# One core's pooled attention with a max-of-two MoE behind it: PE's order from a list scheduler, score groups in bursts, the first K transposed on PE

## The chip, the cores and the metric

The kernel runs on one core of a Trainium2 chip. The metric is device time in microseconds (us) of one execution, as the median of several runs. Engines are named as in the profile: PE (TensorE, matrix products), DVE (VectorE), ACT (ScalarE), POOL (GpSimd) and SP (SyncE, which issues every DMA of this kernel, in order).

## What is computed

Eight batches, eight heads, 1152 keys, head size 64. Queries are averaged in pairs first, so each head has 576 of them. The attention output of all heads, 4608 tokens of 512 values, goes through a small MoE layer.

```python
q_pool = q.reshape(B, H, S // 2, 2, D).mean(axis=3)
scores = np.matmul(q_pool, k.transpose(0, 1, 3, 2)) / np.sqrt(D)
attn = softmax(scores)                      # over the 1152 keys
x = np.matmul(attn, v)                      # -> 4608 x 512
h1, h2 = x @ w1, x @ w2                     # 512 -> 1024
out = np.maximum(h1, h2) @ w_out            # 1024 -> 512
```

The kernel writes max(h1, h2) as relu(x (w1 - w2)) + x w2, so it needs wd = w1 - w2 and w21 = w2 w_out, and never h2 itself.

## The kernel before

A *pair* is two heads of one batch, so there are 32 pairs, four to a batch. A pair is loaded by three DMAs of 576 KB (K, Q, V); POOL casts K to bf16 (L222), adds neighbouring queries (L228) and casts V into vE, which has a column of ones for the softmax sums (L232). K is transposed by a DMA from SP (L225), the pooled Q by six PE transposes and a DVE copy (`qtrans`, L243, L249).

Scores come out transposed, keys on partitions. A *score group* (`scores`) is one tile of 128 keys against 512 queries for both heads, two matmuls in one half each of PE's rows (L263), followed by one exp of 1024 columns on ACT (L275). After nine of these come two groups for the last 64 queries: eight key tiles at once (16 matmuls, one wide exp) and the ninth (2 matmuls, a short exp, L287). That is 11 groups per pair, 352 in all. The groups use two PSUM tiles in turn (`sps`, two banks each).

The product with V (`av_units`) is eight *chunks* of nine matmuls (L305), 128 queries of one head each, and one *rest* of nine for the last 64 queries of both heads (L317), into two banks `av`. DVE divides by the sums (L329 to L345) into xnat. When the fourth pair of a batch is done, five DMA transposes turn xnat into xT (`xtrans`, L369).

The MoE works on blocks of 512 tokens, nine in all, each of which needs the xT of one or two batches. A block is eight hidden units of four matmuls (`hid`, L449) with a relu on DVE (L461), and four output tiles of twelve matmuls (`proj`, L482) with a copy (L496) and two or three stores (L433). In the last blocks ACT takes half of the evacuations (L456, L493). MoE, w21 (L415) and the Q transposes share two banks `mps`.

All instructions are recorded in one program order by class `Plan`, which derives the semaphore waits from the names that an operation reads and writes; each engine then executes its own operations in that order. The order is written out at the end of the function: the loads, casts and transposes of pairs 0 and 1, then all weights (`w_load`), the first Q transpose, then pair by pair the 11 score groups, between which the AV units of the pair before and up to six MoE units are spread by estimated costs. A block enters the queue of MoE units one pair after its last batch is complete, whether or not its xT has landed. So SP's queue begins with the loads of pairs 0 and 1, goes on with w2, its four transposes (L392), w_out and w1, and DVE's with the casts of w2 and w_out and the four subtractions for wd (L403); the copy of the first transposed Q (L249) comes after those.

Of the kernel before, what the change touches and what calls it, by code (L numbers as in the profile page):

```python
# [7 lines left out]
P = 128  # L8
# [5 lines left out]
class Plan:  # L14
# [13 lines left out]
    def op(self, eng, fn, r=(), w=(), dma=None):  # L28
        n = len(self.ops)
        deps = set()  # L30
        raw = set()
        for k in r:
            if k in self.writer:
                deps.add(self.writer[k])
                raw.add(self.writer[k])
# [4 lines left out]
        deps.discard(n)  # L40
        self.ops.append(dict(eng=eng, fn=fn, deps=deps, raw=raw, dma=dma, w=tuple(w)))
# [68 lines left out]

def bass_funnel_attn__then__act_maxout2_kernel(
# [14 lines left out]
    QP = 96  # L126
# [15 lines left out]
    with ctx:  # L142
# [6 lines left out]
        ident = sbuf([QP, QP], BF16, "ident")  # L149
# [19 lines left out]
        w2f = xT[:, :, NTOK - 4096:NTOK - 2048].bitcast(FP32)  # L169
        w2b = xT[:, :, NTOK - 1024:NTOK]  # L170
        w2T = xT[:, :, NTOK - 2048:NTOK - 1024].rearrange("p c (f x) -> p c f x", x=P)
# [11 lines left out]

        mcount = [0]

        def next_m():
            m = mcount[0] % 2
            mcount[0] += 1
            return m

        def setup():
            def ones(g):
# [7 lines left out]
                ident[:, :], ident[:, :], pattern=[[1, QP]], compare_op=ALU.is_equal,  # L200
                fill=0.0, base=0, channel_multiplier=-1), r=["id0"], w=["ident"])

        def load(i):
            b, h0 = i // NHP, 2 * (i % NHP)
            s = i % 2
# [3 lines left out]
                w=[f"kraw{s}"], dma=f"d_k{s}")  # L209
# [3 lines left out]
                w=[f"qraw{s}"], dma=f"d_q{s}")  # L213
# [3 lines left out]
                w=[f"vraw{s}"], dma=f"d_v{s}")  # L217

        def cast(i):
# [3 lines left out]
                kbf[s][:, :, :, :].rearrange("p t h d -> p h t d"), kraw[s][:, :, :, :],  # L223
                1.0, 1.0, ALU.mult, ALU.mult), r=[f"kraw{s}"], w=[f"kbf{s}"])
            op("SP", lambda e: e.dma_start_transpose(  # L225
                kT[v3][:, :, :], kbf[s][:, :, :, :].rearrange("p t h d -> p (t h d)")),
                r=[f"kbf{s}"], w=[f"kT{v3}"], dma=f"d_kT{v3}")
            op("POOL", lambda g: g.tensor_tensor(  # L228
                qp[s][:, :, :, :].rearrange("p u h d -> p h u d"),
                qraw[s][:, :, :, 0, :], qraw[s][:, :, :, 1, :], ALU.add),  # L230
                r=[f"qraw{s}"], w=[f"qp{s}"])
            op("POOL", lambda g: g.tensor_scalar(  # L232
                vE[v3][:, :, :, 0:D].rearrange("p t h d -> p h t d"), vraw[s][:, :, :, :],
                1.0, 1.0, ALU.mult, ALU.mult), r=[f"vraw{s}"], w=[f"vE{v3}"])

        def qtrans(i):
            s = i % 2
            m = next_m()
            mb = mps[m][:, :].bitcast(BF16)

            def pe(e):
                for u in range(QU):
                    last = e.transpose(  # L243
                        mb[:, u * QP:(u + 1) * QP],
                        qp[s][:, u, :, :].rearrange("p h d -> p (h d)"), ident[:, :])
                return last

            op("PE", pe, r=[f"qp{s}", "ident"], w=[f"m{m}"])
            op("DVE", lambda e: e.tensor_copy(qpT[s][:, :], mb[:, 0:SQ]),  # L249
               r=[f"m{m}"], w=[f"qpT{s}", f"m{m}"])  # L250

        gcount = [0]

        def scores(i, g):
# [3 lines left out]
            r = gcount[0] % 2  # L258
# [33 lines left out]
            op("PE", pe, r=[f"kT{ks}", f"qpT{qs}"], w=[f"s{r}"])  # L292
            op("ACT", act, r=[f"s{r}"], w=[w, f"s{r}"])

        def av_units(i):
            b, h0 = i // NHP, 2 * (i % NHP)
            es = i % 2
            vs = i % 3
            xs = b % 2
            c0 = h0 * D  # L300

            def chunk(half, sb):
                def pe(e):
                    for t in range(NT):
                        last = e.matmul(  # L305
                            av[half][:, sb * 66:sb * 66 + 65],
                            eta[es][:, half, t, sb * P:(sb + 1) * P],
                            vE[vs][:, t, half, 0:65],
                            start=(t == 0), stop=(t == NT - 1))
                    return last  # L310
                op("PE", pe, r=[f"eta{es}.{t}" for t in range(NT)] + [f"vE{vs}"],
                   w=[f"av{half}"])

            def rest():
                def pe(e):
                    for t in range(NT):
                        last = e.matmul(  # L317
                            av[0][:, 4 * 66:4 * 66 + 131],
# [197 lines left out]
        for i in range(NPAIR):  # L516
            if i + 2 < NPAIR:
                load(i + 2)
# [87 lines left out]
```

## Time and profile before

| | us |
|---|---|
| median of 3 runs | 530.05 |
| lowest and highest | 528.51, 531.62 |
| the profiled execution | 530.39 |
| its span, first to last instruction | 528.7 |
| PE busy in it | 423.2 |
| ACT busy in it | 325.0 |
| DVE busy, POOL busy | 151.0, 133.3 |

The profile is of one execution; the time that it took and the span of its instructions stand in the table. Busy time counts an engine as working from an instruction's start to its end. Matmuls overlap, so their cost is better read as the distance from one start to the next. The stretches that matter are the beginning, where no scores run yet, the 32 pairs, in which scores, AV and MoE mix, and the end, where two MoE blocks run alone.

### The profile page before, as it was taken

How to read it: one execution, taken by the hardware profiler on the slowest of the kernel's cores; microseconds unless marked ns; L12 is line 12 of the kernel's file. 1: busy time of each engine (PE TensorE's matmuls, PEld its weight loads, DVE VectorE, ACT ScalarE, POOL GpSimd, SP SyncE). 2: the span in 40 equal slices, each digit the busy share in tenths (PEclk: the TensorE clock that was granted, in tenths of full speed). 3: DMA queues.
4: the chain of work that ended last, by engine and by line, in shares of the span. 5: the costliest groups of instructions: out<-in, count | busy, mean ns of one | idle time of the engine just before them, and what ended most of it. 6: DMA issues, size and time to landing. Idle time of an engine off the chain costs nothing.

```text
span 528.7 us, 10621 instructions
## 1 busy us (share of the span) xinstructions
PE 423.2 (80%) x4688; PEld 209.7 (40%) x4688; DVE 151.0 (29%) x330; ACT 325.0 (61%) x365; POOL 133.3 (25%) x105
## 2 busy tenths in 40 slices
PE   0000789849994999789986999799979997899997
PEld 0000245424452445334543455354435443445443
DVE  0107023204222432233222423242224322423221
ACT  0000887937784677757783779477847786674120
POOL 4204233305033233323241422152405032300000
PEclk9999999979997899979997999799979998999999
DMA  8799856049287939975877879695859496702423
GB/s 237 234 274 351 223 149 152 12 112 249 84 207 149 275 45 212 198 190 150 179 217 182 179 170 192 151 241 150 225 131 249 119 200 126 177 21 51 70 65 81
DMA packets 93790, 88.26 MB, mean 167 GB/s; under 512 B 64560, under 2 KB 64560, under 8 KB 93744
## 3 DMA queue, kind: packets, MB, share of 16 engines
q1 hardware_dynamic: 93744, 87.58, 68.4%
q8 instruction: 37, 0.61, 0.5%
q14 instruction: 9, 0.07, 0.0%
HBM read 62.91 MB, written 9.44 MB: 137 GB/s over the span
## 4 chain that ended last, share of the span: by engine, by line
PE 62%; ACT 13%; DMA 13%; SPq 7%; DVE 3%; issue 1%; POOL 0%
PE mps L482 16%; PE sps L263 15%; PE av L305 13%; PE mps L449 13%; ACT eta L275 13%; SPq L369 4%; DMA kT<-kbf 4%; DMA xT<-xnat 3%; PE av L317 2%; DMA stage<-in_moe_w_dram 2%; DMA kraw<-in_k_dram 2%; DVE wd L403 2%; DMA xT<-in_moe_w_dram 2%; PE mps L415 1%; PE mps L243 1%; SPq L392 1%
## 5 line engine op out<-in xcount | busy, mean ns | idle before, releaser
L275 ACT ACTIVATE eta<-sps 128x1024 bf16<-128x1024 f32 x288 | 279.2, 1028 | 157.4 <-PE sps L263 154.5
L263 PE MATMUL sps<-qpT,kT 64*128 64x64 bf16 (+1 forms) x1152 | 136.8, 300 | 62.3 <-DVE qpT L249 43.4
L305 PE MATMUL av<-vE,eta 128*128 128x65 bf16 x2304 | 110.6, 197 | 0.0
L449 PE MATMUL mps<-xT,wd 128*128 128x512 bf16 x288 | 80.7, 413 | 30.1 <-DMA xT<-xnat 30.1
L305 PEld LDWEIGHTS av<-vE,eta 128*128 128x128 bf16 x2304 | 85.0, 99 | 41.9 <-issue 39.8
L263 PEld LDWEIGHTS sps<-qpT,kT 64*128 64x128 bf16 x1152 | 40.1, 94 | 147.9 <-DVE qpT L249 43.6
L222 POOL TENSOR_SCALAR kbf<-kraw 128x1152 bf16<-128x1152 f32 x32 | 38.1, 1191 | 179.7 <-DMA kraw<-in_k_dram 179.7
L461 DVE TENSOR_SCALAR stage<-mps 128x512 bf16<-128x512 f32 x64 | 44.3, 692 | 114.5 <-PE mps L449 114.4
L482 PE MATMUL mps<-wo,stage 128*128 128x512 bf16 x288 | 72.8, 380 | 0.0
L228 POOL TENSOR_TENSOR qp<-qraw 96x768 bf16<-96x768 f32 x32 | 58.1, 1816 | 37.6 <-DMA qraw<-in_q_dram 30.5
L232 POOL TENSOR_SCALAR vE<-vraw 128x1152 bf16<-128x1152 f32 x32 | 36.8, 1150 | 107.4 <-PE av L305 107.4
L449 PEld LDWEIGHTS mps<-xT,wd 128*128 128x128 bf16 x288 | 25.0, 103 | 59.9 <-DMA xT<-xnat 31.4
L496 DVE COPY stage<-mps 128x512 f32<-128x512 f32 x32 | 22.1, 692 | 73.1 <-PE mps L482 73.1
L287 ACT ACTIVATE etb<-sps 128x1024 bf16<-128x1024 f32 x64 | 38.5, 657 | 7.0 <-PE sps L263 7.0
L482 PE MATMUL mps<-w,xT 128*128 128x512 bf16 x144 | 37.1, 380 | 0.0
L329 DVE RECIPROCAL rc<-av 128x6 f32<-128x6 f32 x64 | 12.1, 189 | 87.5 <-PE av L317 69.8
L482 PEld LDWEIGHTS mps<-wo,stage 128*128 128x128 bf16 x288 | 23.9, 98 | 29.6 <-issue 8.6
L249 DVE COPY qpT<-mps 128x576 bf16<-128x576 bf16 x32 | 14.6, 457 | 46.5 <-PE mps L243 46.5
L333 DVE TENSOR_TENSOR xnat<-av,rc 128x256 bf16<-128x256 f32 x64 | 27.2, 424 | 2.2
L317 PE MATMUL av<-vE,etb 128*128 128x131 bf16 x288 | 22.3, 221 | 0.0
L243 PE MATMUL mps<-ident,qp 96*128 96x96 bf16 x192 | 14.1, 212 | 9.3 <-POOL qp L228 9.3
L317 PEld LDWEIGHTS av<-vE,etb 128*128 128x128 bf16 x288 | 16.9, 97 | 5.9 <-issue 5.9
(20 smaller groups left out, 75.1 us busy)
## 6 DMA issues: line engine op xcount, KB each, us to landing
kraw<-in_k_dram SPq DMA_DIRECT2D x32, 576.0 KB, 5.9
qraw<-in_q_dram SPq DMA_DIRECT2D x32, 576.0 KB, 7.8
vraw<-in_v_dram SPq DMA_DIRECT2D x32, 576.0 KB, 8.4
out_dram<-stage SPq DMA_DIRECT2D x24, 192.0 KB, 2.3
out_dram<-stage SPq DMA_DIRECT2D x24, 128.0 KB, 2.5
xT<-in_moe_w_dram SPq DMA_DIRECT2D x1, 2048.0 KB, 8.1
stage<-in_moe_w_out_dram SPq DMA_DIRECT2D x1, 2048.0 KB, 8.6
stage<-in_moe_w_dram SPq DMA_DIRECT2D x1, 2048.0 KB, 13.1
```

Of the source, the lines that this page charges most:

```text
L222: op("POOL", lambda g: g.tensor_scalar(kbf[s][:, :, :, :].rearrange("p t h d -> p h t d"), kraw[s][:, :, :, :], 1.0, 1.0, ALU.mult, ALU.mu ...
L228: op("POOL", lambda g: g.tensor_tensor(qp[s][:, :, :, :].rearrange("p u h d -> p h u d"), qraw[s][:, :, :, 0, :], qraw[s][:, :, :, 1, :], ...
L232: op("POOL", lambda g: g.tensor_scalar(vE[v3][:, :, :, 0:D].rearrange("p t h d -> p h t d"), vraw[s][:, :, :, :], 1.0, 1.0, ALU.mult, ALU. ...
L263: return e.matmul(sps[r][:, half, col:col + n], kT[ks][h:h + 64, t, :], qpT[qs][h:h + 64, lo:lo + n], start=True, stop=True)
L275: return e.activation(eta[es][:, :, g, :], sps[r][:, :, :], EXP, scale=scale)
L287: return e.activation(etb[es][:, t0:t0 + n, :, :].rearrange("p t h c -> p h t c"), sps[r][:, :, 0:n * NB].rearrange("p h (t c) -> p h t c" ...
L305: last = e.matmul(av[half][:, sb * 66:sb * 66 + 65], eta[es][:, half, t, sb * P:(sb + 1) * P], vE[vs][:, t, half, 0:65], start=(t == 0), s ...
L317: last = e.matmul(av[0][:, 4 * 66:4 * 66 + 131], etb[es][:, t, :, :].rearrange("p h c -> p (h c)"), vE[vs][:, t, :, :].rearrange("p h c -> ...
L333: op("DVE", lambda e: e.tensor_tensor(xnat[xs][:, 0:NCH, c:c + D], a[:, 0:NCH * 66].rearrange("p (j c) -> p j c", c=66)[:, :, 0:D], rc[hal ...
L449: last = e.matmul(mps[m][:, :], wd[:, ct, ft * P:(ft + 1) * P], xT[:, ct, n0:n0 + 512], start=(ct == 0), stop=(ct == NC_ - 1))
L461: op("DVE", lambda e: e.tensor_scalar_max(gT[gs][:, ft, :], mps[m][:, :], 0.0), r=[f"m{m}"], w=[f"gT{gs}.{ft}", f"m{m}"])
L482: last = e.matmul(mps[m][:, :], lhs, rhs, start=(part == 0 and j == 0), stop=(part == 2 and j == 3))
```

## The change

PE's order is no longer written out but made by a list scheduler. `Plan.op` now takes a cost and keeps a clock per engine and for the DMA engines, so that `Plan.when` can say when an operation could start. PE's work is put into *jobs* of small units. Two *lanes*, each with one of two PSUM banks `fb`, hold one job at a time; a hidden unit is now two halves of two matmuls, an output tile six units of two. In each step the main loop either emits a burst of two or three score groups, if they can run without a planned stall and ACT's planned lead is short, or the next unit of a lane. Score groups have three PSUM tiles in turn instead of two; `av` and `mps` are gone.

K of pairs 0 to 4 is transposed on PE in two jobs each (`ktrans_pe`), with a DVE copy behind each; later ones by DMA as before. w2 is transposed on PE too (four jobs of eight transposes). w2, w_out and w1 are loaded when pairs 0, 1 and 3 begin, and cast in smaller pieces when the plan sees them landed. K and Q are loaded three pairs ahead and cast two ahead, V two and one; Q of pair 0 is loaded ahead of K, and K of pair 0 is cast on DVE. The transposes to xT and the stores are put into SP's order when the plan sees their data ready. A MoE block is taken up when the plan sees its xT landed and no older block is left.

The core of the diff:

```diff
+    LAT = {"PE": 0.16, "ACT": 0.13, "DVE": 0.1, "POOL": 0.05}
...
+    def when(self, eng, r=(), w=()):
+
+        t = self.free.get(eng, 0.0)
+        for d in self.deps(r, w)[0]:
+            p = self.ops[d]
+            if p["eng"] != eng or p["dma"] is not None:
+                t = max(t, p["seen"] + 0.05)
+        return t
+
...
-        sps = [psum([P, 2, 512], f"sps{g}") for g in range(2)]
-        av = [psum([P, 512], f"av{g}") for g in range(2)]
-        mps = [psum([P, 512], f"mps{g}") for g in range(2)]
+        sps = [psum([P, 2, 512], f"sps{g}") for g in range(3)]
+        fb = [psum([P, 512], f"fb{g}") for g in range(2)]
...
+        def ktrans_pe(i):
+            s = i % 2
+            v3 = i % 3
...
+                def go(e, m, lo=lo, hi=hi):
+                    mb = fb[m][:, :].bitcast(BF16)
+                    for t in range(lo, hi):
+                        last = e.transpose(
+                            mb[:, (t - lo) * P:(t - lo + 1) * P],
+                            kbf[s][:, t, :, :].rearrange("p h d -> p (h d)"), ident[:, :])
+                    return last
+
+                def evac(m, lo=lo, hi=hi):
+                    mb = fb[m][:, :].bitcast(BF16)
+                    dve(lambda e: e.tensor_copy(
+                        kT[v3][:, lo:hi, :].rearrange("p t x -> p (t x)"),
+                        mb[:, 0:(hi - lo) * P]),
+                        [f"f{m}"], [f"kT{v3}", f"f{m}"], 0.7)
+                jobs.append(Job("q", [unit([f"kbf{s}", "ident"], 0.055 * (hi - lo), go)], evac,
+                                ("k", i) if lo else None))
+            return jobs
+
...
         def xtrans(b):
             xs = b % 2
...
                 n0 = b * SQ + j * P
+                under = [key for key, lo, hi in (("w2b", 512, 1536), ("w2T", 1536, 2560),
+                                                 ("w2f", 2560, NTOK))
+                         if n0 < hi and lo < n0 + rows]
                 op("SP", lambda e, rows=rows, n0=n0, j=j: e.dma_start_transpose(
                     xT[:, :, n0:n0 + rows], xnat[xs][0:rows, j, :]),
-                    r=[f"xn{xs}.{j}.{h}" for h in range(H)], 
-                    w=[f"xT.{b}.{j}"] + (["w2f", "w2b", "w2T"] if n0 == 0 else []),
-                    dma=f"d_x{xs}{j}")
+                    r=[f"xn{xs}.{j}.{h}" for h in range(H)],
+                    w=[f"xT.{b}.{j}"] + under,
+                    dma=f"d_x{xs}{j}", cost=0.95, mode="t")
...
-        def moe_units(nb, tail):
+        def moe_jobs(nb, tail):
...
+                def part(kk, ft=ft):
+                    def go(e, m):
+                        for ct in (2 * kk, 2 * kk + 1):
                             last = e.matmul(
-                                mps[m][:, :], wd[:, ct, ft * P:(ft + 1) * P],
+                                fb[m][:, :], wd[:, ct, ft * P:(ft + 1) * P],
                                 xT[:, ct, n0:n0 + 512],
                                 start=(ct == 0), stop=(ct == NC_ - 1))
                         return last
-                    op("PE", pe, r=["wd"] + xkeys(n0, n0 + 512), w=[f"m{m}"])
+                    return unit(["wd"] + xkeys(n0, n0 + 512), 0.432, go)
+
...
+        BURST = 3
+        pe_cost = [0.22] * NT + [0.24, 0.04]
+        act_cost = [0.953] * (NT + 1) + [0.21]
+        groups = [(i, g) for i in range(NPAIR) for g in range(NG)]
+        nxt = 0
+        entered = -1
+        lane = [None, None]
+        av_queue = []
+        q_queue = []
+        w_queue = []
+        moe_queue = []
+        blocks = [((512 * (nb + 1) - 1) // SQ, nb) for nb in range(NBLK)]
+        q_done = set()
+        k_done = set()
+        KPE = 5
+        W_AT = (0, 1, 3)
...
+        def start_k(i):
+            force(("k", i - 2))
+            cast_k(i)
+            if i < KPE:
+                q_queue.extend(ktrans_pe(i))
+            else:
+                later(f"kbf{i % 2}", lambda: (ktrans(i), k_done.add(i)), ("k", i))
+
+        def enter(i):
+            if i + 2 < NPAIR:
+                start_k(i + 2)
+                cast_q(i + 2)
+            if i + 1 < NPAIR:
+                cast_v(i + 1)
+                q_queue.append(qtrans(i + 1))
+            if i + 3 < NPAIR:
+                load_k(i + 3)
+                load_q(i + 3)
+            if i + 2 < NPAIR:
+                load_v(i + 2)
+            if i in W_AT:
+                n = W_AT.index(i)
+                w_load(n)
+
+                def ready():
+                    w_cast(n)
+                    if n == 0:
+                        w_queue.extend(w2t_jobs())
+                    if n == 1:
+                        w_queue.extend(w21_jobs())
+                later(("w2f", "wof", "w1f")[n], ready)
+
...
+        def av_open():
+
+            job, at = av_queue[0]
+            return nxt >= at and plan.when("PE", r=job.units[0][0]) <= now() + 0.1
+
+        def refill():
+
+            if q_queue and plan.when("PE", r=q_queue[0].units[0][0]) <= now():
+                return q_queue.pop(0)
+            if av_queue and (av_open() or nxt >= len(groups)):
+                return av_queue.pop(0)[0]
+            if w_queue and plan.when("PE", r=w_queue[0].units[0][0]) <= now():
+                return w_queue.pop(0)
+            if not moe_queue and blocks and blocks[0][0] in x_done:
+                nb = blocks[0][1]
+                if plan.when("PE", r=xkeys(nb * 512, nb * 512 + 512)) <= now() or nxt >= len(groups):
+                    moe_queue.extend(moe_jobs(blocks.pop(0)[1], nxt >= len(groups)))
+            if moe_queue:
+                if moe_queue[0].kind == "p" and any(l and l.kind == "h" for l in lane):
+                    return None
+                return moe_queue.pop(0)
+            return None
+
+        def burst_now(size):
+
+            todo_g = groups[nxt:nxt + size]
+            if not todo_g:
+                return None, 0.0
+            for p, g in todo_g:
+                if p not in q_done or p not in k_done:
+                    return None, 0.0
+                if p >= 2 and p - 2 not in av_done:
+                    return None, 0.0
+            t = now() + 0.1
+            stall = 0.0
+            n = gcount[0]
+            for kk, (p, g) in enumerate(todo_g):
+                s = plan.when("PE", r=[f"kT{p % 3}", f"qpT{p % 2}"], w=[f"s{(n + kk) % 3}"])
+                stall += max(0.0, s - t)
+                t = max(t, s) + pe_cost[g]
+            return todo_g, stall
+
+        av_done = set()
+
...
+        load_q(0)
+        load_k(0)
+        cast_k(0)
+        cast_q(0)
+        q_queue.extend([qtrans(0)] + ktrans_pe(0))
+        load_k(1)
+        load_q(1)
+        load_v(0)
+        start_k(1)
+        cast_q(1)
+        cast_v(0)
+        load_k(2)
+        load_q(2)
+        load_v(1)
+        turn = 0
+        while nxt < len(groups) or av_queue or moe_queue or blocks or any(lane) or x_wait:
+            flush()
+            lead = plan.free.get("ACT", 0.0) - now()
+            ready = None
+            for size in (3, 2):
+                ready, stall = burst_now(size)
+                if ready and stall <= 0.05:
+                    break
+            first = 0.55
+            for kk in (0, 1):
+                if lane[kk] is None:
+                    lane[kk] = refill()
+            best = None
+            for kk in (turn, 1 - turn):
+                if lane[kk] is not None:
+                    t = plan.when("PE", r=lane[kk].units[0][0], w=[f"f{kk}"])
+                    if best is None or t < best[0] - 0.02:
+                        best = (t, kk, t + lane[kk].units[0][2] - now())
+            if ready and stall <= 0.05 and (best is None or lead < first + best[2]):
+                emit_burst(ready)
+            elif best is not None and (not ready or best[0] <= now() + stall):
+                emit_unit(best[1])
+                turn = 1 - best[1]
+            elif ready:
+                emit_burst(ready)
+            else:
+                plan.free["PE"] = now() + 0.05
+                assert now() < 2000.0, (nxt, entered, lane)
+        plan.free["PE"] = 1e9
+        flush()
 
         plan.solve()
         engines, dmas = plan.sems()
```

## Rows read from the trace of the kernel before

**Rows 1.** The page, part 1: busy time, share of the span and instructions of each engine.

```profile
PE 423.2 (80%) x4688; PEld 209.7 (40%) x4688; DVE 151.0 (29%) x330; ACT 325.0 (61%) x365; POOL 133.3 (25%) x105
```

**Rows 2.** The chain of waits in order of time: start us, us, what.

```profile
0.81 4.39 DMA kraw<-in_k_dram
...
15.04 8.09 DMA xT<-in_moe_w_dram
...
31.52 13.10 DMA stage<-in_moe_w_dram
...
44.65 8.29 DVE wd L403 x4
...
54.02 7.44 ACT eta L275 x8
...
65.83 0.54 PE sps L263
```

**Rows 3.** Timeline of ACT, pair 4: start us, us, engine, line, operation, count, idle before.

```profile
98.55 8.36 ACT L275 ACTIVATE eta<-sps 128x1024 bf16<-128x1024 f32 x9 [0.32 <-PE sps L263]
...
108.31 1.02 ACT L275 ACTIVATE eta<-sps 128x1024 bf16<-128x1024 f32 x1 [0.32 <-PE sps L263]
```

**Rows 4.** Timeline of PE in a pair with MoE work, 128.8 to 141.5 us.

```profile
130.97 0.45 PE L305 MATMUL av<-vE,eta 128*128 128x65 bf16 x9
131.25 1.03 PE L449 MATMUL mps<-xT,wd 128*128 128x512 bf16 x4
132.21 0.39 PE L263 MATMUL sps<-qpT,kT 64*128 64x512 bf16 x2
132.53 0.45 PE L305 MATMUL av<-vE,eta 128*128 128x65 bf16 x9
132.91 0.39 PE L263 MATMUL sps<-qpT,kT 64*128 64x512 bf16 x2
133.24 0.70 PE L317 MATMUL av<-vE,etb 128*128 128x131 bf16 x9
133.77 1.02 PE L482 MATMUL mps<-w,xT 128*128 128x512 bf16 x4
...
137.05 0.43 PE L243 MATMUL mps<-ident,qp 96*128 96x96 bf16 x6
137.31 0.44 PE L305 MATMUL av<-vE,eta 128*128 128x65 bf16 x9
...
138.97 0.41 PE L263 MATMUL sps<-qpT,kT 64*128 64x64 bf16 x16
139.31 0.72 PE L305 MATMUL av<-vE,eta 128*128 128x65 bf16 x18
```

**Rows 5.** By stretches: us, busy us (x instructions) of each engine, granted clock, DMA.

```profile
88.80:108.30 19.50, 16.00 (x249) 9.31 (x248) 4.64 (x15) 18.87 (x23) 6.70 (x6) 1.00 0.22 47
108.30:114.60 6.30, 0.34 (x9) 0.22 (x8) 0.00 (x0) 1.02 (x1) 0.48 (x1) 0.77 0.42 83
114.60:118.50 3.90, 3.86 (x24) 1.51 (x25) 0.69 (x1) 1.26 (x2) 0.00 (x0) 0.50 0.72 205
489.40:524.90 35.50, 35.47 (x160) 14.84 (x160) 8.30 (x12) 6.53 (x11) 0.00 (x0) 1.00 0.34 70
```

**Rows 6.** Waits: engine, line, released by: us in total, times, longest us.

```profile
PE mps L449 <- DMA xT<-xnat: 30.1, 8, 6.0
```

**Rows 7.** Timeline of SP's queue, end of the first batch.

```profile
108.25 6.41 SPq L369 DMA_TRANSPOSE xT<-xnat  x5
```

**Rows 8.** Timeline of PE, two score groups in a row, 80.4 to 81.6 us.

```profile
80.45 0.61 PE L263 MATMUL sps<-qpT,kT 64*128 64x512 bf16 x4
80.99 0.70 PE L317 MATMUL av<-vE,etb 128*128 128x131 bf16 x9
```

**Rows 9.** Timeline of the first 16 us: POOL's add of Q.

```profile
7.43 1.79 POOL L228 TENSOR_TENSOR qp<-qraw 96x768 bf16<-96x768 f32 x1 [1.00 <-DMA qraw<-in_q_dram]
```

**Rows 10.** The page, part 3: DMA queue, packets, MB, share of 16 engines.

```profile
q1 hardware_dynamic: 93744, 87.58, 68.4%
```

More of the change, by code (lines that the diff above doesn't have):

```diff
@@ L26, in __init__, with deps @@
         self.readers = {}
[L28 to L35, printed above, removed]
+        self.free = {}
+        self.dma_free = 0.0
+        self.mode = None
+    def deps(self, r, w):
+        raw = {self.writer[k] for k in r if k in self.writer}
+        deps = set(raw)
         for k in w:
@@ L364, in xtrans @@
+            op("PE", pe, r=[f"kT{ks}", f"qpT{qs}"], w=[f"s{r}"],
+               cost=pe_cost[g], mode="s")
+            op("ACT", act, r=[f"s{r}"], w=[w, f"s{r}"], cost=act_cost[g])
         def xtrans(b):
@@ L419, in go, with evac @@
-                    op("DVE", lambda e: e.tensor_copy(w21[:, ct, :], mps[m][:, :]),
-                       r=[f"m{m}"], w=["w21", f"m{m}"])
-                units.append((1.71, go))
-            return units
+                    return unit([f"w2T{ct}", "wo", "w2T"], 0.432, go)
+                def evac(m, ct=ct):
+                    dve(lambda e: e.tensor_copy(w21[:, ct, :], fb[m][:, :]),
+                        [f"f{m}"], ["w21", f"f{m}"], 0.63)
+                jobs.append(Job("w", [part(kk) for kk in range(4)], evac))
@@ L424, in bass_funnel_attn__then__act_maxout2_kernel @@
+            return jobs
         ocount = [0]
+        held = {}
         def store(t, s):
@@ L546, in bass_funnel_attn__then__act_maxout2_kernel, with part, go @@
[L546 to L552 removed]
+                c0 = n0 + nt * P
+                def part(kk, nt=nt, c0=c0):
+                    def go(e, m):
+                        for j in (2 * kk, 2 * kk + 1):
+                            if j < NC_:
+                                lhs, rhs = xT[:, j, c0:c0 + P], w21[:, j, :]
+                            else:
+                                ft = j - NC_
+                                lhs = gT[gs][:, ft, nt * P:(nt + 1) * P]
+                                rhs = wo[:, ft, :]
+                            last = e.matmul(fb[m][:, :], lhs, rhs,
+                                            start=(j == 0), stop=(j == NC_ + NF - 1))
+                        return last
+                    rd = (["w21"] + xkeys(c0, c0 + P)) if kk < 2 else (
+                        ["wo", f"gT{gs}.{2 * kk - 4}", f"gT{gs}.{2 * kk - 3}"])
+                    return unit(rd, 0.432, go)
@@ new lines, in evac @@
+                def evac(m, nt=nt):
+                    o = ocount[0] % 3
+                    ocount[0] += 1
+                    if o in held:
+                        store(*held.pop(o))
+                    if tail and nt % 2:
+                        op("ACT", lambda e: e.copy(osb[o][:, :], fb[m][:, :]),
+                           r=[f"f{m}"], w=[f"osb{o}", f"f{m}"], cost=0.55)
+                    else:
+                        dve(lambda e: e.tensor_copy(osb[o][:, :], fb[m][:, :]),
+                            [f"f{m}"], [f"osb{o}", f"f{m}"], 0.63)
+                    held[o] = (nb * 4 + nt, o)
@@ new lines, in moe_jobs @@
+                jobs.append(Job("p", [part(kk) for kk in range(6)], evac))
+            return jobs
+        NG = NT + 2
+        BURST = 3
[10 more added lines that the diff above has]
+        blocks = [((512 * (nb + 1) - 1) // SQ, nb) for nb in range(NBLK)]
@@ new lines, in now, with flush @@
+        def now():
+            return plan.free.get("PE", 0.0)
+        def flush():
+            for entry in list(todo):
+                if plan.ops[entry[0]]["seen"] <= now():
+                    todo.remove(entry)
+                    entry[1]()
+            for o in list(held):
+                if plan.ops[plan.writer[f"osb{o}"]]["seen"] <= now():
+                    store(*held.pop(o))
+            for b in list(x_wait):
+                xs = b % 2
+                if plan.ops[plan.writer[f"xn{xs}.{NCH - 1}.{H - 1}"]]["seen"] <= now():
+                    x_wait.remove(b)
+                    xtrans(b)
+                    x_done.add(b)
```

448 lines of the change are left out of this document (222 added, 226 removed).

## The prediction

> **What bounds the kernel now.** I read the page's busy shares first. TensorE (PE) is busy for 80% of the span and no other engine comes near [rows 1], so the first question is what PE does in the other 20%, and the second is what its busy time consists of. The chain of waits answers the first for the beginning: the first exp runs at 54.02 us. Ahead of it stand the load of K (0.81 us, 4.39 long), and then, in one SP queue, w2 (8.09), w_out and w1 (13.10); the chain ends in the subtraction that makes wd on VectorE, from 44.65 to 52.94, behind which the copy of the first transposed Q stands in the DVE queue [rows 2]. Nothing of attention needs wd. The ACT timeline shows what a pair costs where ACT is the limit: from 98.55 to 108.31, 9.76 us for 11 score groups [rows 3]. The PE timeline of a pair with MoE work shows the other limit: there PE has no pause at all and the pair takes 12.7 us (its nine 1024-wide exps would need 9.76). In it nearly every score group stands alone between other matmuls [rows 4]. Finally the view by stretches shows a stall where a batch ends: from 108.30 to 114.60 PE works 0.34 us, and the next 3.9 us run at granted clock 0.50, the 1.2 GHz level, instead of 1.00 [rows 5]. The view of waits puts 30.1 us in 8 such stops on the xT transposes [rows 6]; the SP row shows why: the five transposes of a batch hold SP for 6.41 us [rows 7], and the first MoE block is next in PE's order, ahead of the scores that could have run.
>
> **Prices of PE work, from starts of neighbouring rows.** A score group alone takes 0.32 to the next start, two in a row 0.54 [rows 4, 8], so one group is 0.22 and leaving a run of scores costs 0.10. A chunk ahead of other matmuls takes 0.28, ahead of a score group 0.38: entering a run costs 0.10. So each run of scores pays 0.20 on top. The wide rest group is 0.34 - 0.10 = 0.24, the last one (2 matmuls for 16) 0.03, the 9 "rest" matmuls 0.53, a Q transpose 0.26 [rows 4]. A pair's attention is 9 x 0.22 + 0.24 + 0.03 + 8 x 0.28 + 0.53 + 0.26 = 5.28 us; 32 pairs are 169.0. A MoE block is 20 units of four matmuls at 0.96 - 0.10 = 0.86, 17.2 us; the last two, with nothing else beside them, take 35.50 together [rows 5]: 7 x 17.2 + 35.5 = 155.9. w21 is 8 such units, 6.9. Sum of the work kept: 331.8.
>
> **The change, part by part.**
> *Start.* The weights leave the way: w2, w_out and w1 are loaded at pairs 0, 1 and 3. Q is issued first, then K. The first load of before lands at 5.20, the second, of the same size, at 7.4, when POOL's add of Q starts [rows 2, 9]; with the order turned round K is there at 7.4. Its cast on DVE is about 1 (estimate: half of a wd piece, 2.07 for two inputs), nine transposes and their copies about 1.5. First scores at 10, first exp at 10.5 instead of 54.02. Bounds 9 (cast and transposes of the first half overlap) and 14 (K as late again as the 4.39 of a load, because five loads are now queued at once).
> *Transposes on PE.* 5 x 9 for K and 4 x 8 for w2, 77 of 128 columns. Six of 96 columns take 0.26, so one is 0.058: 4.5 us, bounds 3.4 (0.044) to 9 (six at half clock, 0.116 each). They take 5 K transposes and 4 w2 transposes out of SP's queue; after the start nothing waited for those for long, so I count no gain. The DVE copies they add (14) lie beside PE's two filler banks.
> The Trainium skill, TensorE: Matmul & The Clock Gate, Part 4: PE-mode transpose, puts a 128x128 transpose at about 275 ns inside a kernel; by that figure the 77 would cost 21 us, and the forecast would be 419. The trace disagrees with it for a row of transposes, six in 0.26 us, so it gets no chance of its own.
> *Bursts.* 352 score groups are now in 317 runs (counted in the PE timeline; the rows show the pattern): 63 us of entering and leaving. With three PSUM groups PE can write two while ACT still reads the third. A burst of three fits only where ACT has nearly run dry, since the third group needs the bank that ACT is reading; with fillers at hand the scheduler meets that rarely. Twos alone are 176 x 0.20 = 35, threes alone 24; I take 33. This is 30 us less of PE.
> *Batch ends.* A block's first unit is put into PE's order only when the plan sees its xT landed, and scores go ahead. PE then has MoE work for every free slot: attention leaves 9.76 - 5.28 - 1.03 = 3.45 us per pair, 14 per batch, and a block brings 17.2, so a backlog grows and later blocks start long after their xT. I count the 30.1 us of stops and the half-clock stretches behind them as gone. What is late next: at the first batch nothing is in the backlog. Batch 0 ends at 10.5 + 4 x 9.76 = 49.5; AV of its last pair is released at the sixth group after that (55), the norm ends near 57, the transposes take 6.4 and a landing: first MoE unit at 66.
> *The early gap.* From 10 to 66 PE has 5.7 pairs of scores (5.7 x 3.3 = 18.8), 4.7 of AV (12.8), Q transposes (1.7), the added transposes and w21 (11.4): 44.7 of 56. So 11 us idle, and about 3 more because PE starts at the lower level (at 65.83 the chain still has 0.54 for a score group up to the next start, where 0.32 is normal [rows 2, 4]). 14, bounds 8 to 20.
> *Waits in the queues.* PE runs its order as written; where a real transfer or copy is later than planned, everything behind it waits. The plan has 1.2 for a wd piece; wd took 8.29 for four here [rows 2], 2.07 each. DVE is FIFO, so around pair 4 the Q copy and the norms stand behind wd by up to 6 us. The deeper prefetch gives K and Q about one pair (10 us) of slack for that, and an SP queue held by five transposes delays loads by 6.41 only [rows 7]. Not visible before is how often such a slip reaches PE: bounds 0 and 37 (all stops of before again, 30.1 and some 7 for K and others). I take 3, near the lower end, since in the attention phase PE itself is the slow part and its inputs run ahead.
> *End.* From PE's last start to the span's end 3.8 (528.7 - 524.9 [rows 5]), unchanged.
>
> **Sum.** 10 + 331.8 + 4.5 + 33 + 14 + 3 + 3.8 = 400.1 us of span. The profiled execution took 530.39 with a span of 528.7, so 1.7 lie around it; the median of the runs, 530.05, is 0.3 below that execution, which I ignore. Forecast: 402 us.
>
> **A second way through.** ACT alone would end attention at 10.5 + 32 x 9.76 = 323; behind it come the last AV (2.7), norm and first transpose (about 4), two blocks (35.5) and 3.8: 369. PE's ledger is 31 us longer, so attention may end as late as 354 before it costs anything.
>
> **Rivals.**
> *B, the DMA engines pace attention.* All transfers of before took 68.4% of 16 engines' span, 361.6 us [rows 10]. Of 87.58 MB the change drops about 2.5 (nine transposes), 10 us, and some 12 belong to the last stores: 339 us must pass before attention ends. With the engines full that is 340, under the 354, and costs nothing; at a share of 0.92 it is 369 + 46 = 415, at 0.85 it is 399 + 46 = 445. It decides from a share under 0.96. For it: the stretch without loads in pairs 3 and 4 had a share of 0.22 [rows 5], so SP does leave holes. Against: in that stretch SP sat in front of the transposes of 108.25 [rows 7], waiting for the batch's last norm with the next loads queued behind; the change puts transposes into SP's order only when the plan sees the norm done, and loads two to three pairs ahead. Time 412 to 440, taken as 416.
> *C, the stops come back.* The plan's transfer times are too short, PE waits for xT or K at each batch end and falls to the lower level again: 8 x 3.8 of stop and 8 x about 3.4 of lost clock (half of 6 to 7 us at 0.50) is 58: 460. Against it the backlog, which covers all batches but the first.
> *D, slower than before: half clock through attention.* At the lower level a pair's 5.28 of matmuls become 10.56, with 1.03 of switching 11.6 against 6.3: 5.3 more per pair, and MoE units in such a pair double as well. PE's ledger reaches 530 when 25 of the 32 pairs run so; with all 32 it gives 402 + 170 = 572. It needs PE's short pauses between bursts to be enough to lose the clock. Pairs 3 and 4 of before have just such pauses, PE busy 16.00 of 19.50 us, and the granted clock is 1.00 [rows 5].
> The Trainium skill, TensorE: Matmul & The Clock Gate, A second HAM failure mode: psum-queue depth-cycling, reports a kernel whose short pauses between groups, while it cycles through PSUM banks, make the clock swing; that would be this rival, here from the three-group ring. By that rule the time would be up to the 572; the trace disagrees so far.
> *E, the change doesn't do what it says:* bursts come out as single groups and PE keeps 63 instead of 33: 432, inside the upper part of the range. *F, better than I think:* threes throughout, no early cold: 400.1 - 9 - 6 - 3 + 1.7 = 384.
>
> **How the numbers follow.** My forecast (386 to 412) has 0.60; B 0.20; C 0.08; D 0.03; E 0.04; F 0.05. The range goes from 386 to 436, which leaves out F, C, D and a little of B, about 0.18. A measurement of this kernel tells about 0.5% from no change. Only D and the far end of C reach 527.5: faster 0.96, same 0.01, slower 0.03.
>
> **What would show it.** First exp near 10.5 in the ACT timeline; score runs of four or six matmuls in PE's, some 170 of them; no wait of PE on xT over 2 us after the first block; granted clock 1.00 from about 25 us to the end; attention's last exp between 323 and 354, then 46 to 75 us of MoE alone. If PE is idle for over 30 us between 66 us and the end, the sum was wrong in its waits; if the last exp comes after 360 with DMA at a share under 0.95, B holds.

## The result, and the profile after

The changed kernel takes 435.71 us (median of 4 runs, 435.1 to 439.74); the kernel before took 529.77 beside it. The ratio is 0.825, 95% interval 0.819 to 0.831: 17.5% faster. The forecast was 402, so 34 us of the expected 128 are missing. The time lies at the very end of the range of 386 to 436, and as a ratio (0.825, where 436 of 530.05 is 0.823) just outside it. The profiled execution took 439.74 with a span of 438.0. Its page answers to [rows 1] and [rows 10] (busy time, share, instructions; then the queue's packets, MB, share of 16 engines):

```profile
PE 388.1 (89%) x4714; PEld 205.9 (47%) x4765; DVE 152.7 (35%) x351; ACT 313.1 (71%) x365; POOL 130.4 (30%) x104
...
q1 hardware_dynamic: 83600, 85.05, 78.0%
```

What went as planned is in the timelines of ACT and of PE (start, us, engine, line, work, count, idle before). ACT starts at 11.03 instead of 54.02 [rows 2], and nine K transposes in a row on PE cost 1.05 from their start to the next, at half clock, 0.12 each.

```profile
11.03 8.56 ACT L406 ACTIVATE eta<-sps 128x1024 bf16<-128x1024 f32 x9 [8.95 <-PE sps L394]
```
```profile
16.61 1.12 PE L308 MATMUL fb<-ident,kbf 128*128 128x128 bf16 x9
17.66 1.04 PE L394 MATMUL sps<-qpT,kT 64*128 64x512 bf16 x18
```

What did not is in two stretches (columns as in [rows 5]): up to the last exp at 379.9, and MoE alone. DMA is busy 0.86 of the first. The second has 51 us; from the last exp to the end of the span it is 58, near the short end of the forecast's 46 to 75.

```profile
11.00:382.00 371.00, 335.41 (x4461) 183.78 (x4506) 134.63 (x321) 304.67 (x352) 126.61 (x93) 0.96 0.86 214
382.00:433.00 51.00, 49.78 (x240) 20.75 (x242) 15.32 (x26) 6.53 (x11) 0.00 (x0) 1.00 0.25 64
```

PE's waits on xT [rows 6] are gone from the waits view. But SP's queue has a new line at its top, a transpose that waits for a transpose (engine, line, released by: us, times, longest):

```profile
SPq L435 <- DMA xT<-xnat: 47.1, 26, 8.2
```

To compare whole kernels I add up PE's distances between starts of neighbouring matmuls: to each its price from the prediction (0.216 per 512-wide matmul and so on), 0.105 for each step into or out of a run of scores, the same work once more where the granted clock was 0.50, and what is left over 0.06 is idle. 51 matmul records are missing in the profile of after (4714 against 4765 weight loads); their 11.0 us are put back from idle into work. "Early gap" is idle plus half clock up to 80 us. Work and switching are therefore counts times the prediction's prices; what tests the prices is the rounding line, by which they overstate. The table is of the profiled executions: after's is 4.0 us above its median and e7's 2.5 below, so what an edit is worth is better read from the medians below.

| us | forecast | after | e6 | e12 | e7 | e8 |
|---|---|---|---|---|---|---|
| first matmul | 10 (first scores) | 7.9 | 7.4 | 7.6 | 7.6 | 7.5 |
| work, with added transposes | 336.3 | 334.5 | 334.4 | 334.4 | 334.4 | 335.3 |
| in and out of score runs | 33 | 32.8 | 32.8 | 32.8 | 33.2 | 58.4 |
| early gap: idle + half clock to 80 us | 14 | 15.2 + 10.2 | 15.1 + 7.9 | 13.9 + 10.0 | 14.3 + 9.0 | 12.7 + 6.8 |
| later idle + half clock | 3 | 27.7 + 8.0 | 15.5 + 1.8 | 15.4 + 3.1 | 8.5 + 0 | 9.4 + 0 |
| rounding | | -3.2 | -1.9 | -2.2 | -2.6 | -2.8 |
| last start to end | 3.8 | 5.1 | 4.7 | 4.7 | 5.1 | 4.7 |
| span | 400.1 | 438.0 | 417.6 | 419.7 | 409.5 | 432.1 |

Work, switching and the end are within 2 us of the forecast. The miss is in two lines: 11 in the early gap, 33 later. Of the 11, 1.8 lie before the first scores at 10.4, which the forecast's first line contains.

### The profile page after: what moved, and what is told of

It is laid out like the page before. It is cut to its first block, busy times and chain, and to the rows that moved or that the text cites. A ratio compares the mean times of both kernels' runs of the same rounds, so it can differ in the third digit from the quotient of the medians.

```text
span 438.0 us, 10776 instructions
## 1 busy us (share of the span) xinstructions
PE 388.1 (89%) x4714; PEld 205.9 (47%) x4765; DVE 152.7 (35%) x351; ACT 313.1 (71%) x365; POOL 130.4 (30%) x104
## 3 DMA queue, kind: packets, MB, share of 16 engines
q1 hardware_dynamic: 83600, 85.05, 78.0%
## 4 chain that ended last, share of the span: by engine, by line
PE 64%; DMA 15%; DVE 7%; ACT 6%; SPq 3%; issue 2%; POOL 1%; DVEq 0%
PE fb L571 17%; PE fb L333 15%; PE sps L394 13%; PE fb L541 13%; ACT eta L406 6%; DMA xT<-xnat 4%; DMA kT<-kbf 4%; PE fb L344 4%; DMA qraw<-in_q_dram 3%; DMA out_dram<-stage 3%; DVE stage L555 2%; DVE xnat L361 2%; DVE stage L587 1%; SPq L256 1%; SPq L435 1%
## 5 line engine op out<-in xcount | busy, mean ns | idle before, releaser
L394 PE MATMUL sps<-qpT,kT 64*128 64x64 bf16 (+1 forms) x1152 | 108.0, 298 | 12.5 <-ACT eta L406 6.1
L333 PE MATMUL fb<-vE,eta 128*128 128x65 bf16 x2304 | 97.0, 199 | 11.9 <-DVE stage L587 11.2
L333 PEld LDWEIGHTS fb<-vE,eta 128*128 128x128 bf16 x2304 | 86.5, 101 | 37.8 <-DVE stage L587 12.4
L249 POOL TENSOR_SCALAR kbf<-kraw 128x1152 bf16<-128x1152 f32 x31 | 35.7, 1150 | 159.7 <-DMA kraw<-in_k_dram 159.7
L541 PE MATMUL fb<-xT,wd 128*128 128x512 bf16 x259 | 68.8, 384 | 6.6 <-DVE rc L357 3.7
L571 PE MATMUL fb<-wo,stage 128*128 128x512 bf16 x281 | 70.7, 380 | 0.9 <-issue 0.8
L555 DVE TENSOR_SCALAR stage<-fb 128x512 bf16<-128x512 f32 x64 | 43.3, 689 | 56.6 <-PE fb L541 56.6
L571 PEld LDWEIGHTS fb<-wo,stage 128*128 128x128 bf16 x288 | 25.1, 98 | 36.6 <-issue 11.9
L571 PE MATMUL fb<-w,xT 128*128 128x512 bf16 x132 | 35.3, 380 | 4.3 <-DVE rc L357 3.1
L361 DVE TENSOR_TENSOR xnat<-fb,rc 128x256 bf16<-128x256 f32 x64 | 27.2, 425 | 2.2
L344 PE MATMUL fb<-vE,etb 128*128 128x131 bf16 x288 | 22.6, 224 | 0.0
```

The costliest lines, as they stand in the source:

```text
L249: op("DVE" if i == 0 else "POOL", lambda g: g.tensor_scalar(kbf[s][:, :, :, :].rearrange("p t h d -> p h t d"), kraw[s][:, :, :, :], 1.0, ...
L333: last = e.matmul(fb[m][:, sb * 66:sb * 66 + 65], eta[es][:, half, t, sb * P:(sb + 1) * P], vE[vs][:, t, half, 0:65], start=(t == 0), stop ...
L344: last = e.matmul(fb[m][:, 4 * 66:4 * 66 + 131], etb[es][:, t, :, :].rearrange("p h c -> p (h c)"), vE[vs][:, t, :, :].rearrange("p h c -> ...
L361: dve(lambda e: e.tensor_tensor(xnat[xs][:, 0:NCH, c:c + D], a[:, 0:NCH * 66].rearrange("p (j c) -> p j c", c=66)[:, :, 0:D], rc[half][:, ...
L394: return e.matmul(sps[r][:, half, col:col + n], kT[ks][h:h + 64, t, :], qpT[qs][h:h + 64, lo:lo + n], start=True, stop=True)
L541: last = e.matmul(fb[m][:, :], wd[:, ct, ft * P:(ft + 1) * P], xT[:, ct, n0:n0 + 512], start=(ct == 0), stop=(ct == NC_ - 1))
```

## The experiments

**Theory X: a wait that the change added.** In the diff, `xtrans` writes the names of the weight buffers that lie under xT. Before, only the piece at column 0 did ([rows 7]: five transposes, 6.41 us of SP). Now every piece whose columns overlap does, which is 36 of the 40, so nearly each transpose writes a name that the one before has just written, and must wait until that one has landed. SP works in order, so loads, K transposes and stores wait too. Theory W puts the stops on the ring of three output buffers, theory B (the prediction's rival) on the DMA engines. W's place in after is this:

```profile
173.36 2.25 SPq L526 DMA_DIRECT2D out_dram<-stage  x4
...
176.50 0.69 DVE L587 COPY stage<-fb 128x512 f32<-128x512 f32 x1 [2.74 <-DMA out_dram<-stage]
...
177.25 3.47 PE L333 MATMUL fb<-vE,eta 128*128 128x65 bf16 x63 [3.01 <-DVE stage L587]
...
181.70 0.28 ACT L418 ACTIVATE etb<-sps 128x128 bf16<-128x128 f32 x1 [7.46 <-PE sps L394]
```

Ahead of it stand the five transposes of a batch. The first was issued at 152.87 and landed at 164.52; the second was issued at 164.54, and these last four hold SP 7.37 us. The stores come behind them; DVE's copy waits for the store, PE for the copy, and ACT, last in the row, for PE: 7.46.

*e1: more output buffers.*

```diff
-        osb = [stage[:, NC_ * F + s * E:NC_ * F + (s + 1) * E] for s in range(3)]
+        osb = [stage[:, NC_ * F + s * E:NC_ * F + (s + 1) * E] for s in range(8)]
```

> The changed kernel with eight output staging buffers instead of three. Theory W (PE's written order stands behind output copies whose buffer is still being stored, because SP issues the stores late, behind the xT transposes): the 11 to 12 us of PE waits on the output copy go, and the three half-clock stretches near them, about 5 us of lost clock: 420 to 426 instead of 435.7. Rival B (the DMA engines pace attention): the bytes are the same and so is the time, 433 to 438.

Measured 434.37 (433.07 to 436.04), ratio 0.821, not apart from after. W falls: the copies no longer wait for stores (9.2 us in three waits in after, none in e1), PE's waits on the copies go from 11.2 to 0.7, and the time stays, so it does not hang on them. The head of that chain, the transposes in SP, is unchanged. The SP timeline of e1 shows it, against [rows 7]:

```profile
292.06 14.50 SPq L435 DMA_TRANSPOSE xT<-xnat  x5
306.61 0.59 SPq L228 DMA_DIRECT2D kraw<-in_k_dram  x1
```

Five transposes hold SP 14.50 us where they held it 6.41, and the next load stands behind them.

*e6: the wait taken away.* A name is written only by the first piece that touches its buffer, which is all that is needed, as SP issues them in order.

```diff
+        undone = set()
...
-                         if n0 < hi and lo < n0 + rows]
+                         if n0 < hi and lo < n0 + rows and key not in undone]
+                undone.update(under)
```

> The changed kernel with one difference: a transpose to xT waits for the readers of the weight buffers that lie under xT only where it is the first to touch such a buffer; the later ones no longer wait for the landing of the one before. Theory X (that wait, 47.1 us of SP in 26 waits, holds the loads and K transposes behind it and so paces attention): the five transposes of a batch hold SP for 6.5 us instead of up to 14.5, the last exp comes at 340 to 350 instead of 382, and the time falls by 25 to 35 us to 401 to 411. Rival B (the 16 DMA engines themselves are the limit, at a share of 0.86): the bytes are the same, the time stays within 5 us of 435.7.

Measured 418.58 (415.92 to 420.84), ratio 0.790 (0.786 to 0.795): 17 us faster than after, less than the 25 to 35 expected, far more than B's 5. The new line is gone from SP's waits, the five transposes of a batch take 6.42 to 9.15 (the row below is one of the shorter) where they took 9.84 to 19.03, the last exp ends at 348.6 instead of 379.9, and later idle and half clock fall from 35.7 to 17.3. Packets and bytes are those of after, to the last packet, but the share of the attention stretch is now 0.99:

```profile
320.38 7.48 SPq L438 DMA_TRANSPOSE xT<-xnat  x5
```
```profile
11.00:349.00 338.00, 321.44 (x4383) 171.82 (x4382) 128.90 (x309) 304.36 (x352) 127.39 (x93) 0.97 0.99 232
```

The 17 us are not SP's stops alone. `Plan` takes its clocks from the same names, so the scheduler reckons with the wait: from 130.7 us of after on, the order of PE differs between after and e6. Worked out from the kernels' code, a waiting transpose takes 4.2 us on the plan's clocks (2.4 in the trace), which makes a K transpose late behind each batch, and scores are put off until then. On these clocks pairs 14, 18, 22 and 26 of after (counted from 0) take 17 to 21 us each and PE ends at 448; in e6 these pairs take 10 and PE ends at 407. Measured, from first exp to first exp, they take 16.3 to 17.7 in after, and in e6 no pair after 80 us takes over 12.3. In after PE stops for a K transpose once (pair 5, 3.9 us), and the K of pairs 15, 19, 23 and 27 landed 6.4 to 7.5 us before their first exp. So much of the 17 us lies in the order that was written around the wait; no run here separates it from the stops.

*e9: the same wait put into the kernel before.*

```diff
-                    w=[f"xT.{b}.{j}"] + (["w2f", "w2b", "w2T"] if n0 == 0 else []),
+                    w=[f"xT.{b}.{j}"] + (["w2f", "w2b", "w2T"] if n0 == 0 else ["w2f"]),
```

> The kernel before with that wait put in: every transpose to xT names a weight buffer as written, so each waits for the landing of the one before. Theory X: the five transposes of a batch hold SP for some 14 us instead of 6.41, PE and the loads behind them wait for it in each of 8 batches, and the time rises by 25 to 60 us, to 555 to 590. Rival B: under 5 us, since no transfer is added.

Measured 560.1, ratio 1.058 (1.053 to 1.063): 31 us slower, of which PE's idle is 23.5 (101.4 to 124.9) and half clock 6.9 (20.0 to 26.9). The five transposes of a batch hold SP 10.88 to 12.42 us (the first batch is shown), and the stops of [rows 6] grow from 30.1 to 44.7:

```profile
108.33 10.88 SPq L369 DMA_TRANSPOSE xT<-xnat  x5
```
```profile
PE mps L449 <- DMA xT<-xnat: 44.7, 8, 9.7
```

So one name in a write list costs 17 us in one kernel and 31 in the other. In e9 the orders of PE and SP are those of before, so its 31 us are the wait alone; the 17 are the wait and the order planned around it. To that extent X is shown, by its removal and by its addition.

**What is left: output buffers or lanes.** e7 is e6 with eight output buffers and a rule that at most one lane takes MoE work while an AV job is queued.

```diff
             if moe_queue:
+                if av_queue and any(l and l.kind in "hp" for l in lane):
+                    return None
```

> As e6_under_once, with eight output staging buffers and with MoE allowed only one of the two lanes while an AV job is queued. If what is left after e6 is the blocking of AV by two output tiles at once, pairs come out at 9.8 to 10.5 us each and the time is 3 to 6 us under e6; if PE's own ledger (work, switching, the early gap) is the limit, it is within 2 us of e6.

Measured 413.74 (411.24 to 414.88), ratio 0.782 (0.779 to 0.785). It is 4.8 us under e6, and no kernel here is faster. e12 is e7 without the rule:

> e7_lanes without the lane rule, so the kernel with the wait on the transpose before taken away (e6_under_once, 418.6 us) and 8 output buffers instead of 3. Theory L: the lane rule makes most of the 4.8 us between e6_under_once and e7_lanes, since the AV of a pair is what frees its exp buffer: 417 to 419. Theory O: the output buffers make most of it, since with three of them the copy of an output tile waits for a store that is queued in SP: 413 to 415.

Measured 420.71 (417.67 to 421.44), ratio 0.792 (0.787 to 0.797): the buffers give nothing, as in e1 (the orders of PE and SP are those of e6); the rule gives 7. ACT's waits for scores fall with it from the first line to the second (e12, then e7), and PE's later idle from 15.4 to 8.5. That this comes from exp buffers coming free earlier is argued, not shown.

```profile
ACT eta L406 <- PE sps L394: 42.2, 32, 8.7
```
```profile
ACT eta L406 <- PE sps L394: 23.1, 22, 8.7
```

**Bursts.** e5 is after with one score group at a time, e8 is e12 with the same edit.

```diff
-            for size in (3, 2):
+            for size in (1,):
```

> The changed kernel with the scheduler emitting one score group at a time, on the same ring of three. If entering and leaving a run of scores costs 0.20 us, the runs go from 156 to nearly 352 and the time rises by 30 to 39 us, to 466 to 475. If PE is not what the end hangs on (rival B), most of it disappears beside transfers: under 450.

Measured 440.04, ratio 0.832 (0.828 to 0.835): 4 us slower, not 30. The score runs rise from 156 (100 of four matmuls, 29 of eighteen, 21 of six) to 281 and switching from 32.8 to 59.0, but idle and half clock fall by nearly as much: PE was waiting in after anyway.

> As e6_under_once with eight output staging buffers, but score groups one at a time. With the supply of K no longer the limit, PE's ledger should be: the runs of scores double and the time is 15 to 26 us over e6. If PE is still not the limit, it is within 6 us of e6, as the single groups were within 5 us of the change.

Measured 434.97 (433.83 to 435.67), ratio 0.821 (0.819 to 0.824): 16 slower than e6, 14 slower than e12. Without that name the price shows; of the 25.6 us more switching PE's smaller gaps give some 13 back (table). So the same part of the change is worth 4 us or 14, by what else binds. Read the other way, the name costs 5 us with single groups (440.04 against 434.97). Up to 322 us e5 and e8 have one order of PE, and e5 has the wait at full length:

```profile
SPq L435 <- DMA xT<-xnat: 47.1, 26, 5.0
```

e8, without the wait and with eight buffers, is ahead by 3.0 us at 132 us and by 3.0 at 322: in that order, at 11.1 us per pair, the same 47.1 us of waiting in SP cost nothing.

**The start and K on PE.** e4 does one part alone: the kernel before, with the weights loaded after pair 0 and cast later, K transposed by DMA as it was.

```diff
-        w_load()
         qtrans(0)
...
+            if i < 3:
+                (w_load, w_cast, w_sub)[i]()
```

> The kernel before with one part of the change alone: the three weight matrices are loaded after the first pair and cast one and two pairs later, the PE order is otherwise as before. If the start is worth what the prediction's step says, the first exp comes at 11 to 15 us instead of 54.02 and the time falls by 36 to 42 us to 488 to 494. If the loads only move and are paid again in pairs 1 to 4, less than 25 us.

Measured 509.37, ratio 0.963 (0.959 to 0.967). The first exp comes at 11.28, 43 us earlier, but the gain is 20: the K transpose of pair 2 stands behind three weight loads, and holds SP 11.33 us itself.

```profile
31.44 11.33 SPq L225 DMA_TRANSPOSE kT<-kbf  x1
```
```profile
48.13 0.61 PE L263 MATMUL sps<-qpT,kT 64*128 64x512 bf16 x2 [16.47 <-DMA kT<-kbf]
```

e10 asks the same of the best kernel: e7 with `KPE = 1` instead of 5, so that K of pairs 1 to 4 goes by DMA.

> The best version so far (e7_lanes, 413.7 us, last exp at about 333) with K on PE undone for pairs 1 to 4: only the K of pair 0 is transposed on PE, the others by DMA in SP's queue. Theory K: the PE transposes earn their place early, because a K transpose in SP's queue waits behind the loads that fill the DMA rings (in e7_lanes the first one, of pair 5, holds SP for 11.07 us at 46.19); with four more of them between 10 and 45 us the pairs 2 to 5 start late by some 3 to 10 us together, minus 36 transposes of 0.058 (2.1 us of PE): 416 to 424 us. Rival: PE has slack early (15 us idle before 80 us), and the DMA transposes lie beside it: 411 to 414 us, no difference.

Measured 421.37 (419.51 to 423.39), ratio 0.793 (0.787 to 0.800): 7.6 slower than e7. K on PE is worth that much, although pair 7 starts 15 us later (98.1 against 83.2): the backlog of MoE work pays part of it. Two K transposes hold SP 13.56 us behind the loads, and PE stops (SP's timeline, then PE's):

```profile
15.06 13.56 SPq L256 DMA_TRANSPOSE kT<-kbf  x2
```
```profile
29.79 0.61 PE L394 MATMUL sps<-qpT,kT 64*128 64x512 bf16 x2 [11.32 <-DMA kT<-kbf]
```

In the other direction, e2 is after with `KPE = 8`, e11 is e7 with `KPE = 6`.

> The changed kernel with K of pairs 0 to 7 transposed on PE instead of 0 to 4. Theory W: the K transpose of pair 5, which SP holds for 11.65 us beside the load of w1, no longer stops PE for 4 us at 61 us, and the half-clock stretch of 10.2 us behind it (5 us lost) goes; 27 transposes add 1.6 us: 427 to 430. Rival B: three DMA transposes fewer of 27, 3 to 4 us at most: 431 to 434.

Measured 444.66 (443.81 to 445.5), ratio 0.840: 9 slower than after. In it one pair takes 20.7 us (62.0 to 82.7), with a PE stop of 4.22 at 65.9, ahead of w21's matmuls. Its PE order differs from after's from 41.6 us on, and the wait on the transposes was still in it; the cause stays open.

> e7_lanes with the K of pair 5 on PE as well. Theory G: what is left of the early gap comes from the K of pair 5, whose DMA transpose is queued behind w1 in SP's queue; on PE it is off that queue, pairs 4 and 5 (11.8 and 12.0 us in e7_lanes) come down to about 10, and the time falls by 2 to 4 us: 410 to 412. Rival: K itself lands late because w1 takes the DMA engines (POOL's cast of K waits up to 8.4 us for the load), so the transposition is late on PE as well and the next DMA transposes inherit the full rings: 413 to 416, no difference.

Measured 413.83 (412.8 to 418.45), ratio 0.782: no difference. The stop of pair 5 is gone, and the K of pair 6 has taken its place in SP's queue (10.88 us at 54.60). Which K comes behind w1 is not what sets the early gap.

## Why the prediction was wrong

*The step that failed* is "Waits in the queues", 3 us taken from bounds of 0 and 37. Measured: 27.7 idle and 8.0 half clock after 80 us, 35.7, within those bounds, at the far end; PE's idle from 66 us on is 30, where over 30 was the sign for it. I reasoned that an SP queue held by five transposes delays loads "by 6.41 only", a length read from a kernel in which the transposes follow each other without waiting. The diff on the same page adds a name to the write lists of 36 of the 40. The part-by-part names the waits that the change removes at batch ends and never asks what the new `under` list makes each transpose wait for, nor what the scheduler, which plans with the same list, makes of it. With e6, 17 of the 34 missing us go with that name. e7 takes off 5 more (7 against e12) by the lanes' order, which no step of mine had a term for. The 12 that remain lie mostly in the early gap.

*Rival B* (0.20) showed its sign word for word: last exp at 379.9, after 360, with DMA at 0.86. Its own formula at 0.86 gives 339 / 0.86 + 46 = 440, and the profiled execution took 439.74. That the two meet is luck: the formula ends attention at 394 and leaves 46 behind it, where 379.9 and 58 were measured. The mechanism, SP leaving holes in the DMA engines, was right in kind. What I held against it was when transposes are put into SP's queue; what they wait for once they are at its head decided. The point I relied on slipped as well: up to the last exp SP's transposes to xT wait 26.3 us for DVE in after, and 5.0 in e6. It is not that the DMA engines were too slow: in e6 the same 83,600 packets pass at a share of 0.99, attention ends at 348.6 (333.2 in e7), and B's point, 0.96, has been crossed to the side where it costs nothing. Nor is the 339 a fixed load: the times of the same packets add up to 342 us of 16 engines in after (78.0% of 438.0) and to 360 in e6 (86.2% of 417.6).

*The early gap* was 14 with bounds of 8 and 20, measured 25.4 in after and 23 in e6 and e7. Its idle part was 11, measured 14 to 15. The half clock was mis-sized: 3, measured 8 to 10. In after PE runs at half rate until 23.4 us and falls to 0.50 again at 64.3 and at 84.8; e7 falls once more, at 64.1. The first MoE unit, forecast for 66, comes at 89.0: K transposes hold SP 11.65 (at 47.53), 5.77 and 4.85 us behind w1 and the loads, and the five xT transposes of the first batch start only at 74.09, for 9.84. So SP was the late engine there as well. In e7 the unit comes at 84.19 and the gap is nearly the same; e11 says that one K more or less does not matter. Over the first 80 us DMA's share in after is 1.05 (packets that overlap can take it past 1), so full DMA engines may set this gap; no run tests it.

*What held.* First exp 11.0 (10.5 forecast). Work 334.5 (336.3), and with it the added transposes, 0.056 from start to start at the full clock, though each lasts 0.22 by itself. Switching 32.8 (33), since there are 156 runs ("some 170"). The stops on xT are gone from PE. The end, 58 us behind the last exp. Rival E (no bursts) gave 30 us; e8 has 25.6 of switching and 14 of time, since part of it falls into gaps.

*Rival D*, the half clock, did not decide but did appear. After the start, four half-clock stretches come with a stop: one of 10.2 us from 64.3 with the stop of 3.99 that begins at 60.9, and three of 3.4 us after stops of 3.16, 2.90 and 4.39. One does not:

```profile
79.00:84.80 5.80, 4.36 (x91) 2.82 (x88) 1.70 (x6) 5.80 (x8) 1.15 (x1) 1.00 0.80 122
84.80:91.60 6.80, 5.77 (x53) 3.48 (x56) 1.05 (x2) 4.58 (x6) 2.04 (x2) 0.50 0.95 278
```

Before it PE worked 4.36 of 5.80 us, in bursts that wait 0.4 to 0.5 for ACT with no MoE work to put between, and then ran 6.80 us at the 1.2 GHz level; in [rows 5] it worked 16.00 of 19.50 and kept 2.4 GHz. The Trainium skill, TensorE: Matmul & The Clock Gate, section "A second HAM failure mode: psum-queue depth-cycling", describes such a fall between short pauses. The traces agree with it in part. e6 and e12 have the same pauses and fall at 84.5 and 83.8, but e7 has them too, 0.40, 0.53 and 0.51, and in its profiled execution the clock stays at 1.00 from 71.0 to the end of the matmuls:

```profile
80.59 0.41 PE L394 MATMUL sps<-qpT,kT 64*128 64x64 bf16 x16 [0.53 <-ACT eta L406]
81.51 0.20 PE L394 MATMUL sps<-qpT,kT 64*128 64x64 bf16 x2 [0.51 <-ACT eta L406]
```

So the pauses alone do not decide, and what does stays open. The fall in after cost some 3 us (half of 6.80), not the 5.3 per pair of D.

## What to carry to other kernels

When a change touches the write list of an operation on an in-order queue, work out what that operation now waits for, and then everything queued behind it, and everything that is planned from the same list; a duration read from the old trace holds only while its waits are the same. A term with bounds of 0 and 37 is the forecast's weakest; the diff, line by line, is what narrows it, and a low share on a shared resource is a reason to look for the queue that feeds it. What an edit on one engine is worth depends on whether that engine is the limit: bursts gave 4 us with that name in the write lists and 14 without. A scheduler that keeps clocks carries a forecast of its own, which can be read before any run: on them PE ends at 448 in after, 407 in e6 and 402 in e7, where the spans are 438.0, 417.6 and 409.5.

## What the runs showed of the hardware

- A DMA transpose to xT lands 2.5 us after its issue (median in before and after; 4.1 in e6). Issued without waiting, five take 6.41 to 7.44 us of SP in before and 6.42 to 9.15 in e6. Waiting for each landing makes 10.88 to 12.42 of the five in e9, and up to 19.03 in after, where the first can land 11.65 us after its issue.
- A DMA transpose issued behind large loads holds its queue: one takes 1.35 us of SP at 85.67 in after, 11.65 behind w1, 11.33 in e4, 13.56 for two in e10.
- The view by stretches showed a granted clock of 1.00 for the first 20 us of after, yet three chunks in a row took 1.67 us there, 0.56 each where 0.28 is normal [rows 4]. The record begins at the first change (23.4 us), so a 1.00 ahead of it says nothing:

```profile
20.39 1.67 PE L333 MATMUL fb<-vE,eta 128*128 128x65 bf16 x27
```
